# A second dense layer computed by Strassen's seven block products, its output product too

## The chip, the cores and the metric

The kernel runs on one core of one Trainium2 chip. The metric is the device time of one execution in microseconds. Engines of the core are called by the profile's names: PE (matmul) with its weight loads PEld, DVE (vector), ACT (scalar and tables), POOL (GpSimd), and SP, which here issues the DMAs.

## The reference, cut to what matters

```python
# q, k, v: (4, 8, 576, 64) fp32; all weights fp32
attn = softmax(q @ k.T / 8, block-causal mask, blocks of 64) @ v
x = attn.transpose(0, 2, 1, 3).reshape(2304, 512)
h = x @ w_in                       # 512 -> 2048
x = (h - tanh(h)) @ w_out          # 2048 -> 512      "first layer"
xn = x / sqrt(mean(x * x) + 1e-6) * rms_g
g, val = xn @ w_gate, xn @ w_val   # 512 -> 1536 each  "second layer"
out = (g * sigmoid(g) * val) @ w_out2   # 1536 -> 512
```

The weights arrive as float64, so each piece of them (512 numbers a partition, 512 KB) is first converted to fp32 by integer and float operations on DVE and ACT (`convert`).

## The kernel before, in words

**Precision.** Each fp32 operand is held as two fp32r parts, high and low, and each product is three matmuls: high by high, high by low, low by high (`gemm_out`, `product`). Making the two parts is called a split: ACT writes the high part (`rnd`, L100), DVE or POOL subtracts it for the low one (`lo`, L105).

**Tiling.** The 2304 tokens form six groups of 384 (`NG`, `TG`), a group three tiles of 128. The first layer takes group after group; in each, 16 steps (`J1`) of 128 hidden columns: four products of 384 columns for the hidden block (L799 to L801), tanh, and three token tiles' output products of 512 columns into three accumulators (L682 to L684). The attention of later groups is woven between these matmuls by the class `Attn`. In group 0 the first layer's weights are converted; later groups load the split weights again from DRAM copies (`w1d`), two steps ahead, into rings of four buffers.

**The second layer** takes pairs of groups. Its 12 hidden blocks (`J2`) need w_gate, w_val and w_out2. In group 5 of the first layer and in the first pair (`unit_piece`, `unit_sums`, `out_piece`) these are converted: 24 pieces of gate and value weights and 12 of output weights. In the first pair (`plain`) gate and value products are the ordinary ones for each of the two groups. Meanwhile each block's seven Strassen weight combinations are written to DRAM (`w2d`). The second and third pair (`fast`) use them: one hidden block needs 7 block products of 2 x 3 matmuls of 384 columns for both groups together, where the ordinary way needs 8. The Strassen blocks are: rows of the product are gate and value, its columns the two groups. The output product is the ordinary one in all pairs: `out2`, with all 12 split output weight blocks (`wout`) kept in SBUF, 512 columns a matmul, one group first and then the other (`later` holds the second group's hidden blocks until then).

**Order.** PE's order is that of the program text. For the other engines the compiler's scheduler orders instructions, except those pinned (`pin`). Each engine runs its queue in order. All DMAs are issued by SP in one order; an SP entry that waits holds back the ones behind it.

Of the kernel before, what the change touches and what calls it, by code (L numbers as in the profile page):

```python
# [50 lines left out]
EARLYOUT = 6  # L51
LATEOUT = (1, 2, 4, 5, 7, 8)
# [39 lines left out]
def build(ctx, tc, q, k, v, w_in, w_out, w_gate, w_val, w_out2, rms_g, ident_in, out):  # L92
# [19 lines left out]
    w2d = [[drm.tile([128, 2, n], F32, name=f"w2d_{n}_{j}") for j in range(J2)] for n in (768, 1024)]  # L112
# [68 lines left out]
    env["ev"] = wk  # L181
# [393 lines left out]
    with tc.manual_schedule(engines={PE.engine}):  # L575
# [110 lines left out]
        def out1(s, t):  # L686
# [8 lines left out]
            if j == J1 - 1:  # L695
                c = g * TT + t
                x2s = env["ev"].tile([128, DM], F32, name="x2s", tag="x2s")
# [9 lines left out]
        xin = {}  # L707

        def xn_a(n, t):
            c = n * TT + t  # L710
            x = w2a.tile([128, DM], F32, name="xin", tag="xin", bufs=4)
            SP.dma_start(out=x, in_=x2d[c * 128:(c + 1) * 128, :])
            pin(DVE.scalar_tensor_tensor(x, x, rinv[:, c:c + 1], g_bc, ALU.mult, ALU.mult))
            xin[n, t] = x

        def xn_b(n, t):
            x = xin.pop((n, t))
            xh, xl = xt("B", n)
            ps = env["t"].tile([128, 512], F32, name="t", tag="t")
            for kk in range(KD):  # L720
                PE.transpose(ps[:, kk * 128:(kk + 1) * 128], x[:, kk * 128:(kk + 1) * 128], ident)
            tv = ps.rearrange("p (k c) -> p k c", k=KD)
            hv, lv = (a[:, :, t * 128:(t + 1) * 128] for a in (xh, xl))
# [3 lines left out]
        w2 = {}  # L727
        wout = {}
        full = {}

        def out_piece(j):
            pool = w2a if j < EARLYOUT else w2b
            wout[j] = [pool.tile([128, 512], F32R, name=f"wo_{j}_{y}") for y in "hl"]
            convert(stage(rows_(w_out2, j)), *wout[j])

        def unit_piece(j, part):
            if part == 0:
                full[j] = w0.tile([128, 2, 512], F32, name="fu", tag="fu", bufs=4)
            f = full[j]
            convert(stage(cols((w_gate, w_val)[part], j)), f[:, part])  # L740
            if part == 1:
                w2[j] = w = w0.tile([128, 2, 2, 512], F32R, name="wu", tag="wu", bufs=4)
                rnd(ACT, w[:, 0], f)
                lo(DVE, w[:, 1], f, w[:, 0])

        def unit_sums(j):

            f = full.pop(j).rearrange("p g (k c) -> p (g k) c", k=2)
            g_l, g_u, v_l, v_u = (f[:, n] for n in range(4))
            o = w0.tile([128, 4, 256], F32, name="fs", tag="fs")  # L750
            POOL.tensor_tensor(out=o[:, 0], in0=v_u, in1=v_l, op=ALU.add)
            POOL.tensor_tensor(out=o[:, 2], in0=g_u, in1=v_u, op=ALU.subtract)
            POOL.tensor_tensor(out=o[:, 1], in0=o[:, 0], in1=g_u, op=ALU.subtract)
            POOL.tensor_tensor(out=o[:, 3], in0=g_l, in1=o[:, 1], op=ALU.subtract)
            w = w0.tile([128, 2, 4, 256], F32R, name="ws", tag="ws")
            pin(ACT.activation(out=w[:, 0], in_=o, func=AF.Copy))
            lo(DVE, w[:, 1], o, w[:, 0])
            pin(SP.dma_start(out=w2d[0][j], in_=w2[j].rearrange("p x g c -> p x (g c)")[:, :, 0:768].bitcast(F32)))
            SP.dma_start(out=w2d[1][j], in_=w.rearrange("p x g c -> p x (g c)").bitcast(F32))

        pieces = []
        for j in range(4):
            pieces += [lambda j=j: unit_piece(j, 0), lambda j=j: unit_piece(j, 1)]
            if j:
                pieces += [lambda n=n: out_piece(n) for n in ((0, 1), (2, 3), (4, 5))[j - 1]]
# [3 lines left out]
        w2a = None  # L769
        nld = J1  # L770
        for s in range(NSA):
            g, j = divmod(s, J1)
            if j == 0:
                if g == 2:
# [3 lines left out]
                    env["x4"] = x4.__enter__()  # L778
                base, goal = att.pos, att.goal(g)
# [40 lines left out]
            if s:  # L820
# [4 lines left out]
                gts.pop(s - 1)  # L825
            if j == J1 - 1:
                while att.pos < goal:
                    att.step()
                if g == NG - 2:
                    x4.__exit__(None, None, None)  # L830
                    sat.close()
                    sw = ExitStack()
                    w2a = sw.enter_context(tc.tile_pool(name="w2a", bufs=1, side="right"))
                    sw0 = ExitStack()
                    w0 = sw0.enter_context(tc.tile_pool(name="w0", bufs=1, side="right"))
                    env["stg"] = sw0.enter_context(tc.tile_pool(name="st2", bufs=3, side="right"))
                    g_bc = w2a.tile([128, DM], F32, name="g_bc")
                    SP.dma_start(out=g_bc, in_=rms_g.rearrange("(o d) -> o d", o=1).broadcast_to([128, DM]))
                    sev = ExitStack()
                    env["ev"] = sev.enter_context(tc.tile_pool(name="ev", bufs=3, side="right"))  # L840
            if g == NG - 1:
                if j == 5:
                    rms(0, 15)
# [212 lines left out]
```

## Time and profile before

| what | value |
|---|---|
| median of 3 runs | 1082.54 us (1081.65 to 1083.05) |
| the profiled execution | 1080.89 us |
| its span, first to last instruction | 1079.1 us |
| PE busy | 1049.6 us, 97% |
| DVE, ACT, POOL busy | 741.7, 568.2, 253.3 us |
| granted PE clock | 0.995 of 2.4 GHz |
| DMA | 238.43 MB |

Busy shares are means over stages. The stages on the span's clock, read from the last square of each group's output (L700) and PE's first `fast` product of a pair: group 1 of the first layer ends near 257 us, group 2 near 371, group 3 near 463, group 4 near 561, group 5 near 630; the first pair of the second layer ends near 791, the second near 935, the third near 1074, five us before the span's end.

### The profile page before, as it was taken

The page shows a single profiled execution, that of the slowest core. Times are in us where ns is not written, and L with a number is a line of the kernel's source. Part 1 is how long each engine was busy: PE and PEld are TensorE (multiplying, and loading weights), DVE is VectorE, ACT ScalarE, POOL GpSimd, SP SyncE. Part 2 cuts the span into 40 slices and gives each one's busy share as a digit, 9 for nine tenths or more (in the row PEclk, how much of TensorE's full clock was granted, in tenths as well). Part 3 has the DMA queues.
Part 4 walks back from the last instruction along what each step waited for, and adds up shares of the span by engine and source line. Part 5 has one row for each costly group of instructions (what it writes and reads, how often), then busy time and mean ns, then how long its engine had stood idle before and what let it go on. Part 6 is the DMA issues. An engine that isn't in the chain of part 4 may idle for free.

```text
span 1079.1 us, 16811 instructions
## 1 busy us (share of the span) xinstructions
PE 1049.6 (97%) x5588; PEld 932.4 (86%) x5588; DVE 741.7 (69%) x1559; ACT 568.2 (53%) x1307; POOL 253.3 (23%) x372
## 2 busy tenths in 40 slices
PE   7799999999999999999999989999999999999998
PEld 5576668998888999999998979999899998899986
DVE  5888767777777856576657779997455566555552
ACT  5877747667666755476556576563322223322221
POOL 5531201123233223143211013436011021110010
PEclk9999999999999999999999999999999999999999
DMA  9798888978668887775569976894745555154501
GB/s 220 229 292 295 256 292 263 295 209 247 165 176 204 228 236 219 225 227 176 180 228 402 343 263 238 292 327 186 302 151 183 194 205 186 43 216 187 198 24 36
DMA packets 179639, 238.43 MB, mean 221 GB/s; under 512 B 109152, under 2 KB 134368, under 8 KB 174944
## 3 DMA queue, kind: packets, MB, share of 16 engines
q1 hardware_dynamic: 179552, 237.35, 68.2%
q8 instruction: 45, 0.74, 0.3%
q14 instruction: 42, 0.34, 0.1%
HBM read 184.88 MB, written 52.43 MB: 220 GB/s over the span
## 4 chain that ended last, share of the span: by engine, by line
PE 82%; DVE 7%; DMA 4%; ACT 4%; issue 2%; SPq 0%; POOL 0%; DVEq 0%; POOLq 0%; ACTq 0%
PE acc L682 8%; PE acc L684 8%; PE acc L683 8%; PE gv L873 8%; PE gv L872 7%; PE gv L874 7%; PE t L799 5%; PE t L801 5%; PE t L800 5%; PE t L465 5%; PE t L506 3%; PE acc L692 3%; PE t L530 2%; PE t L559 2%; DMA w<-w1d_i 2%
## 5 line engine op out<-in xcount | busy, mean ns | idle before, releaser
L799 PE MATMUL t<-xh,w 128*128 128x384 f32 x384 | 137.8, 359 | 0.0
L801 PE MATMUL t<-xh,w 128*128 128x384 f32 x384 | 129.9, 338 | 0.0
L800 PE MATMUL t<-xl,w 128*128 128x384 f32 x384 | 129.5, 337 | 0.0
L480 ACT ACTIVATE pt<-pt,stat 128x64 f32<-128x64 f32 (+2 forms) x144 | 80.4, 560 | 45.0 <-DVE pt L478 43.7
L100 ACT ACTIVATE gh<-gt 128x384 fp32r<-128x384 f32 x116 | 60.5, 521 | 74.8 <-DVE gt L813 34.7
L682 PE MATMUL acc<-w,gh 128*128 128x512 f32 x240 | 99.1, 413 | 0.3 <-ACT gh L100 0.3
L684 PE MATMUL acc<-w,gl 128*128 128x512 f32 x240 | 95.3, 397 | 1.1 <-DVE gl L105 1.1
L683 PE MATMUL acc<-w,gh 128*128 128x512 f32 x240 | 94.7, 395 | 0.0
L105 DVE TENSOR_TENSOR gl<-gt,gh 128x384 fp32r<-128x384 f32 x116 | 73.5, 633 | 24.3 <-ACT gh L100 24.0
L682 PE MATMUL acc<-wo_h,gh 128*128 128x512 f32 x216 | 85.7, 397 | 0.4 <-ACT gh L100 0.4
L684 PE MATMUL acc<-wo_h,gl 128*128 128x512 f32 x216 | 85.3, 395 | 0.0
L683 PE MATMUL acc<-wo_l,gh 128*128 128x512 f32 x216 | 84.9, 393 | 0.0
L799 PEld LDWEIGHTS t<-xh,w 128*128 128x128 f32 x384 | 72.4, 189 | 3.6 <-issue 0.7
L100 ACT ACTIVATE pp<-t 128x512 fp32r<-128x512 f32 (+6 forms) x152 | 64.2, 437 | 21.1 <-PE t L506 20.4
L478 DVE TENSOR_SCALAR_CACHE_REDUCE pt<-t 128x64 f32<-128x64 f32 (+2 forms) x144 | 64.0, 449 | 16.2 <-PE t L465 15.0
L800 PEld LDWEIGHTS t<-xl,w 128*128 128x128 f32 x384 | 72.5, 189 | 2.2
L801 PEld LDWEIGHTS t<-xh,w 128*128 128x128 f32 x384 | 72.1, 188 | 0.0
L959 POOL TENSOR_TENSOR gs<-c,c 128x384 f32<-128x384 f32 x24 | 24.4, 1015 | 201.4 <-ACT c L958 201.4
L813 DVE TENSOR_TENSOR gt<-t,gt 128x384 f32<-128x384 f32 x80 | 44.2, 553 | 39.5 <-ACT gt L807 39.3
L506 PE MATMUL t<-ident,pt 128*128 128x128 f32 x400 | 65.8, 274 | 3.7 <-POOL pt L493 2.4
L807 ACT ACTIVATE gt<-t 128x384 f32<-128x384 f32 x96 | 46.6, 485 | 40.4 <-PE t L801 40.0
L956 ACT ACTIVATE gt<-c 128x384 f32<-128x384 f32 x24 | 12.6, 526 | 102.1 <-DVE c L955 102.1
(155 smaller groups left out, 2827.4 us busy)
## 6 DMA issues: line engine op xcount, KB each, us to landing
w<-w1d_i SPq DMA_DIRECT2D x80, 512.0 KB, 4.6
w<-w1d_o SPq DMA_DIRECT2D x64, 512.0 KB, 4.3
wb<-w2d SPq DMA_DIRECT2D x24, 1024.0 KB, 4.8
wa<-w2d SPq DMA_DIRECT2D x24, 768.0 KB, 6.3
st<-in_moe_w_out SPq DMA_DIRECT2D x28, 512.0 KB, 4.9
w2d<-ws SPq DMA_DIRECT2D x12, 1024.0 KB, 6.0
w2d<-wu SPq DMA_DIRECT2D x12, 768.0 KB, 5.7
st<-in_moe_w_in SPq DMA_DIRECT2D x16, 512.0 KB, 4.8
```

Source lines behind the costliest of these rows:

```text
L100: ACT.activation(out=o, in_=i, func=AF.Copy)
L480: ACT.activation(out=pt[:, 0:keys], in_=pt[:, 0:keys], func=AF.Exp, scale=-1.0, bias=least, accum_out=st[:, 8 + ti:9 + ti])
L506: PE.transpose(t[:, (j - a) * 128:(j - a + 1) * 128], pt[:, j * 128:(j + 1) * 128], ident)
L682: PE.matmul(acc, lhsT=gh[:, c], rhs=wh, start=first, stop=False)
L683: PE.matmul(acc, lhsT=gh[:, c], rhs=wl, start=False, stop=False)
L684: PE.matmul(acc, lhsT=gl[:, c], rhs=wh, start=False, stop=last)
L799: PE.matmul(h, lhsT=wh[:, c], rhs=xh[:, kk], start=(kk == 0), stop=False)
L800: PE.matmul(h, lhsT=wh[:, c], rhs=xl[:, kk], start=False, stop=False)
L801: PE.matmul(h, lhsT=wl[:, c], rhs=xh[:, kk], start=False, stop=(kk == KD - 1))
L872: PE.matmul(ps, lhsT=wh[:, c], rhs=xh[:, kk], start=(kk == 0), stop=False)
L873: PE.matmul(ps, lhsT=wh[:, c], rhs=xl[:, kk], start=False, stop=False)
L874: PE.matmul(ps, lhsT=wl[:, c], rhs=xh[:, kk], start=False, stop=(kk == nk - 1))
```

## The change

All three pairs now use the seven-product scheme for gate and value (`fast`), and the output product uses it as well (`tail`): over 6 pairs of hidden blocks (`JH`), 7 products of 6 blocks, each for three token tiles with matmuls of 256 columns; the seven left operands are hidden blocks or sums of them made by POOL (`sums`, `sub`), split while the products run; `combine` adds the products into the two groups' outputs on DVE, and half rows of 256 columns are stored. The output weights are no longer held in SBUF: their seven combinations lie in DRAM (`wod`), and each product loads its 6 blocks (1.5 MB) into one of three weight slots (`ws`), which hold the gate and value weights too.

The conversion moves. 11 units (6 of output weights, 5 of gate and value weights; a unit is two pieces, four POOL sums and a split of 1792 columns whose subtraction POOL makes) are converted in groups 2, 3 and 4 of the first layer, as 44 items, four a unit: 10 in group 2, 16 in group 3, 18 in the first 12 steps of group 4; the results are sent to DRAM. The 7 gate and value units of `DIRECT` are converted in group 5 and the first pair, straight into slots or kept buffers; they are written to DRAM for the later pairs (`keep`). The first pair's normalised tokens are loaded, combined and transposed during group 5 (`PREP`).

```diff
+JH = J2 // 2
+DIRECT = (0, 1, 2, 3, 4, 6, 8)
+            def send(self, eng, half):
+                n = slice(3, 7) if half else slice(0, 3)
+                w = env["wsp"].tile([128, 2, 4, 256], F32R, name="wc", tag="wc")[:, :, 0:n.stop - n.start]
+                self.split_part(w, eng, half)
+                if self.kind == "g":
+                    pin(SP.dma_start(out=w2d[self.j][:, :, n], in_=w.bitcast(F32)))
+                    return
+                for y in range(2):
+                    pin(SP.dma_start(out=wod[:, n, self.j, 256 * y:256 * y + 256], in_=w[:, y].bitcast(F32)))
...
+            if 2 <= g < NG - 1:
+                nit = {2: 0, 3: 10, 4: 26}[g] + (j + 1) * {2: 10, 3: 16, 4: 24}[g] // J1
+                while 44 - len(items) < min(nit, 44):
+                    items.pop(0)()
...
-        gvp = ctx.enter_context(tc.tile_pool(name="gvp", bufs=4, space=PSUM))
-        env["t"] = ctx.enter_context(tc.tile_pool(name="tb", bufs=1, space=PSUM))
-        accp = ctx.enter_context(tc.tile_pool(name="accb", bufs=1, space=PSUM))
+        gvp = ctx.enter_context(tc.tile_pool(name="gvp", bufs=8, space=PSUM))
...
+        ORDER = (4, 1, 2, 5, 6, 7, 3)
+        def tail(p):
+            def split(m):
+                i, j = steps[m]
+                f = left[i](j)
+                gh, gl = ([wk.tile([128, TG], F32R, name=n, tag=n) for n in ("gh", "gl")] if m % 2 else
+                          [temp(n, F32R) for n in ("c21", "c22")])
+                rnd(ACT, gh, f)
+                lo(DVE, gl, f, gh)
+                parts.append((gh, gl))
+                if i == 2:
+                    sub(f, f, GS[1][j])
...
+            for n, i in enumerate(ORDER):
+                q = p * NQ + J2 + n
+                load_slot(q + 2)
+                w = slots.pop(q).rearrange("p x n c -> p (x n c)")
+                ps = [bank()[:, 0:256] for t in range(TT)]
+                for j in range(JH):
+                    m = n * JH + j
+                    if m + 3 < len(steps):
+                        split(m + 3)
+                    gh, gl = parts[m]
+                    wh, wl = (w[:, 512 * j + 256 * y:512 * j + 256 * y + 256] for y in range(2))
+                    for t in range(TT):
+                        gemm_out(ps[t], gh, gl, wh, wl, t, j == 0, j == JH - 1)
+                for t in range(TT):
+                    combine(i, t, ps[t])
+                if p + 1 < NG // 2:
+                    if n == 0:
+                        nx = pair_x()
+                    if n < 2:
+                        for k in range(4):
+                            pair_b(n, k, nx, bank)
...
+        for p in range(NG // 2):
+            for j in range(J2):
+                if p or j:
+                    load_slot(p * NQ + j + 2)
...
+                if p == 0:
+                    if j + 3 in direct:
+                        if j + 3 >= 5:
+                            direct[j + 3].piece(1)
+                        direct[j + 3].sums()
+                    if j + 4 in DIRECT[5:]:
+                        direct[j + 4].load()
+                        direct[j + 4].piece(0)
+                fast(p * NQ + j, j, x)
...
+                if j > JH:
+                    if j == JH + 1:
+                        sums(0)
+                    sums(j - JH)
+            x = tail(p)
```

PE, where the first pair goes over to its output products. Before, matmuls of 512 columns into accumulators that stay for twelve blocks:

```order
L682 MATMUL acc_8898<-wo_h,gh 128x512
L683 MATMUL acc_8898<-wo_l,gh 128x512
L684 MATMUL acc_8898<-wo_h,gl 128x512
L682 MATMUL acc_8902<-wo_h,gh 128x512
L683 MATMUL acc_8902<-wo_l,gh 128x512
L684 MATMUL acc_8902<-wo_h,gl 128x512
```

After, matmuls of 256 columns into a bank of the ring `gv`; `ws` is the weight slot, `c` and `gh`/`gl` the two parts of the left operand:

```order
L685 MATMUL gv<-ws,c_8961 128x256
L683 MATMUL gv<-ws,c_8960 128x256
L684 MATMUL gv<-ws,c_8960 128x256
L685 MATMUL gv<-ws,c_8961 128x256
L683 MATMUL gv<-ws,gh 128x256
L684 MATMUL gv<-ws,gh 128x256
```

The first pair has 216 of the former in the one and 378 of the latter in the other; so have the second and the third.

SP, late in group 3 of the first layer. Before, loads of the first layer's weights (`w`) stand among the attention's (`kr`, `qr`, `vr`) alone:

```order
L641 DMA w_5168<-w1d_i_107 128x1024
L270 DMA qr<-in_q 32x6x32 x3
L651 DMA w_5084<-w1d_o_122 128x1024
L270 DMA kr<-in_k 32x18x32 x4
L641 DMA w_5224<-w1d_i_108 128x1024
L651 DMA w_5170<-w1d_o_123 128x1024
```

After, stores of converted combinations (`wod<-wc`) and loads of weights to convert (`st`) stand between them:

```order
L642 DMA w_5624<-w1d_i_100 128x1024
L758 DMA wod<-wc 128x3x256 x2
L652 DMA w_5560<-w1d_o_115 128x1024
L126 DMA st<-in_moe_w_gate 128x4x256
L126 DMA st<-in_moe_w_val 128x4x256
L642 DMA w_5703<-w1d_i_85 128x1024
L652 DMA w_5626<-w1d_o_116 128x1024
```

The store waits for POOL's subtraction into `wc`; the next step's weights are issued behind it.

DVE, in the third hidden block of the first pair. Before, the conversions of gate, value and output weights with the products' multiplications (L911) between them:

```order
L139 TENSOR_SCALAR cv<-cv 128x512
L140 SCALAR_TENSOR_TENSOR cv<-cv,cu 128x512
L141 SCALAR_TENSOR_TENSOR fu<-st,cv 128x512
L911 TENSOR_TENSOR gt<-gv,gt 128x384
L105 TENSOR_TENSOR ws<-fs,ws 128x1024
L105 TENSOR_TENSOR wu<-fu,wu 128x1024
```

After, the subtraction of a unit's split (L739) and the eight operations of `fast` (L1008 to L1019):

```order
L739 TENSOR_TENSOR ws<-fu,ws 128x768
L1008 TENSOR_TENSOR c_8153<-gv,c_8151 128x384
L1009 TENSOR_TENSOR c_8152<-gv,c_8153 128x384
L1013 TENSOR_TENSOR c_8151<-gv,c_8151 128x384
L1011 TENSOR_TENSOR c_8154<-gv,c_8152 128x384
L1012 TENSOR_TENSOR c_8153<-gv,c_8153 128x384
L1015 TENSOR_TENSOR c_8152<-gv,c_8152 128x384
L1018 TENSOR_TENSOR c_8153<-gv,c_8153 128x384
L739 TENSOR_TENSOR ws<-fs,ws 128x1024
L1019 TENSOR_TENSOR g_2_8217<-c_8153,gt 128x384
```

A block of the first pair now has these eight DVE operations in place of two multiplications and a split (`gl`); fewer conversions stand beside them.

## Rows read from the trace of the kernel before

**Rows 1.** The page: busy time by engine, and the chain by engine.
```profile
PE 1049.6 (97%) x5588; PEld 932.4 (86%) x5588; DVE 741.7 (69%) x1559; ACT 568.2 (53%) x1307; POOL 253.3 (23%) x372
...
PE 82%; DVE 7%; DMA 4%; ACT 4%; issue 2%; SPq 0%; POOL 0%; DVEq 0%; POOLq 0%; ACTq 0%
```

**Rows 2.** Windows by stage: stretch, then busy us per engine, clock, DMA share, GB/s.
```profile
257.00:371.00 114.00, 109.77 (x635) 100.41 (x634) 88.54 (x248) 78.57 (x215) 35.27 (x54) 0.99 0.74 195
371.00:463.00 92.00, 92.00 (x504) 84.23 (x503) 57.87 (x137) 53.10 (x124) 24.09 (x36) 1.00 0.83 233
463.00:561.00 98.00, 97.65 (x550) 89.63 (x549) 62.68 (x143) 58.35 (x134) 29.46 (x44) 1.00 0.59 191
561.00:630.00 69.00, 67.62 (x339) 59.57 (x338) 53.74 (x90) 43.93 (x81) 4.03 (x4) 1.00 0.92 344
630.00:791.00 161.00, 157.13 (x842) 146.43 (x841) 125.95 (x172) 85.60 (x146) 56.93 (x56) 1.00 0.73 262
791.00:935.00 144.00, 143.78 (x767) 133.79 (x766) 84.86 (x143) 37.93 (x75) 21.30 (x24) 1.00 0.45 168
935.00:1074.00 139.00, 138.78 (x722) 128.83 (x720) 73.25 (x124) 32.27 (x63) 12.19 (x12) 1.00 0.35 131
```

**Rows 3.** Windows again, of two short stretches where DMA or DVE is fullest.
```profile
570.00:600.00 30.00, 29.50 (x146) 25.82 (x145) 21.15 (x35) 17.95 (x32) 3.19 (x4) 1.00 1.04 402
660.00:690.00 30.00, 30.00 (x166) 29.06 (x165) 29.27 (x38) 18.23 (x31) 13.88 (x12) 1.00 0.90 323
```

**Rows 4.** Timeline of PE near 800 us: start, duration, instruction.
```profile
799.68 0.34 PE L872 MATMUL gv<-xh,wa 128*128 128x384 f32 x1
...
806.51 0.39 PE L682 MATMUL acc<-wo_h,gh 128*128 128x512 f32 x1
...
808.60 0.34 PE L872 MATMUL gv<-xh,wa 128*128 128x384 f32 x1
```

**Rows 5.** Timeline of PE near 766 us, around transposes.
```profile
765.81 1.69 PE L988 MATMUL gv<-ident,xn 128*128 128x128 f32 x14
767.26 0.48 PE L682 MATMUL acc<-wo_h,gh 128*128 128x512 f32 x1
```

**Rows 6.** PE groups by shape: count, busy us, mean ns, idle before.
```profile
L872 PE MATMUL gv<-xh,wb 128*128 128x384 f32 x192 | 64.6, 336 | 0.0
...
L539 PE MATMUL t<-pp,vp 128*128 128x256 f32 x32 | 9.0, 280 | 0.0
```

**Rows 7.** DVE groups by shape.
```profile
L140 DVE SCALAR_TENSOR_TENSOR cv<-cv,cu 128x512 int32<-128x512 int32 x68 | 53.3, 785 | 4.3
...
L139 DVE TENSOR_SCALAR cv<-cv 128x512 f32<-128x512 f32 x68 | 35.8, 527 | 9.5 <-ACT cv L136 8.9
...
L961 DVE TENSOR_TENSOR gt<-c,gt 128x384 f32<-128x384 f32 x24 | 23.2, 967 | 2.5
L105 DVE TENSOR_TENSOR gl<-gs,gh 128x384 fp32r<-128x384 f32 x36 | 21.6, 599 | 36.6 <-ACT gh L100 36.6
...
L141 DVE SCALAR_TENSOR_TENSOR fu<-st,cv 128x512 int32<-128x512 int32 x24 | 17.8, 742 | 0.3
...
L955 DVE TENSOR_TENSOR c<-gv,c 128x384 f32<-128x384 f32 x24 | 13.4, 559 | 0.9
...
L105 DVE TENSOR_TENSOR xl<-gv,xh 128x512 fp32r<-128x512 f32 x18 | 11.3, 685 | 0.9 <-ACT xh L100 0.7
```

**Rows 8.** ACT groups by shape.
```profile
L136 ACT ACTIVATE cv<-st 128x512 f32<-128x512 f32 x68 | 45.4, 667 | 17.6 <-DVE fu L141 6.6 <-DVE wo_l L105 3.2 <-DMA st<-in_moe_w_gate 2.5
...
L100 ACT ACTIVATE wu<-fu 128x1024 fp32r<-128x1024 f32 x12 | 12.7, 1060 | 11.2 <-PE gv L874 5.1 <-issue 4.9 <-DVE fu L141 1.1
```

**Rows 9.** POOL groups by shape.
```profile
L959 POOL TENSOR_TENSOR gs<-c,c 128x384 f32<-128x384 f32 x24 | 24.4, 1015 | 201.4 <-ACT c L958 201.4
...
L751 POOL TENSOR_TENSOR fs<-fu 128x256 f32<-128x256 f32 x12 | 14.0, 1171 | 137.8 <-DVE ws L105 124.0 <-DMA xin<-x2d 13.8
```

**Rows 10.** Timeline of PE near 634 us: the longest wait of the handover.
```profile
636.57 0.66 PE L721 MATMUL t<-ident,xin 128*128 128x128 f32 x4 [2.19 <-DVE xl L105]
```

More of the change, by code (lines that the diff above doesn't have):

```diff
@@ L705, in rms @@
             pin(DVE.reciprocal(rinv[:, a:z], rinv[:, a:z]))
[L707 to L723, printed above, removed]
+        sources = {("g", j): (cols(w_gate, j), cols(w_val, j)) for j in range(J2)}
@@ new lines, in away, with first, second, third @@
+        def away(units, eng):
+            items = []
+            for n, c in enumerate(units):
+                def first(n=n, c=c):
+                    if n == 0:
+                        c.load()
+                    c.piece(0)
+                def second(n=n, c=c):
+                    c.piece(1)
+                    if n + 1 < len(units):
+                        units[n + 1].load()
+                def third(c=c):
+                    c.sums()
+                    c.send(eng, 0)
+                items += [first, second, third, lambda c=c: c.send(eng, 1)]
+            return items
@@ L724, in xn_b @@
             rnd(ACT, hv, tv)
             lo(DVE, lv, tv, hv)
[L727 to L765, printed above, removed]
+        def tbank():
+            return env["t"].tile([128, 512], F32, name="t", tag="t")
+        slots = {}
+        def slot(q):
+            slots[q] = tp.tile([128, 2, 7, 256], F32R, name="ws", tag="ws", bufs=3)
+            return slots[q]
+        items = away([Convert("o", j) for j in range(JH)]
+                     + [Convert("g", j) for j in range(J2) if j not in DIRECT], POOL)
@@ new lines, in build @@
+                    for n in range(3):
+                        items[4 * n + 2] = direct[n].sums
+                        items[4 * n + 3] = lambda n=n: direct[n].split(slot(n), POOL)
+                    items[14:16] = []
+                    items[16:18] = []
+            if g == NG - 1:
+                for k, f in PREP:
+                    if k == j:
+                        f()
+                if j == 14:
+                    direct[0].keep()
+                while len(items) > 16 - (j + 1):
+                    items.pop(0)()
@@ L995, in build @@
[L995 to L1009 removed]
+            POOL.tensor_tensor(out=result(1, j), in0=c12, in1=c22, op=ALU.mult)
@@ new lines, in fast, with sub, sums @@
+            DVE.tensor_tensor(c21, prod(2, xd, 0), c21, ALU.add)
+            DVE.tensor_tensor(result(0, j), c21, gt, ALU.mult)
+        GS = [{}, {}]
+        def sub(o, a, b, op=ALU.subtract):
+            POOL.tensor_tensor(out=o, in0=a, in1=b, op=op)
+        def sums(j):
+            for s in GS:
+                if j not in s:
+                    s[j] = sums_pool.tile([128, TG], F32, name=f"gs{j}_{0 if s is GS[0] else 1}")
+            sub(GS[0][j], G[1][j], G[1][j + JH], ALU.add)
+            sub(G[1][j], G[0][j], G[1][j])
+            sub(GS[1][j], GS[0][j], G[0][j])
@@ L1023, in build @@
[L1023 to L1035 removed]
+                if p == 0 and j == JH:
+                    sw0.close()
+                    sums_pool = sw.enter_context(tc.tile_pool(name="sums", bufs=1, side="right"))
```

331 lines of the change are left out of this document (178 added, 153 removed).

## The prediction

> **What bounds the kernel now.** I read the busy times first, then the chain, then windows cut at the stages, then PE's timeline. PE is busy 97% of the span and is 82% of the chain [rows 1]. A busy PE can still be a slow one, so the cadence is what counts. From the first 384-column matmul shown to the first 512-column one, 39 matmuls start in 6.83 us, 0.175 us each; the nine of 512 columns that follow take 2.09 us, 0.232 each [rows 4]. The windows say where PE stands idle: 4.2 us in group 2, 0.4 in groups 3 and 4, then 1.4 in group 5, 3.9 in the first pair and 0.4 in the two pairs after it [rows 2]. The reader should see that groups 3 and 4 have DVE and ACT at only 58 to 64%, while the first pair has DVE at 78%, and at 98% from 660 to 690 us [rows 3]: room is in the first layer, load is in the first pair. The clock is full in nearly all rows and stays out of the sum. So time goes mostly where PE work goes, plus the waits that the moved conversions make or take away.
>
> **PE work, part by part.** The durations of a group by shape hold the pipeline's depth: 336 ns against a cadence of 175, so 161 ns of depth. A 256-column matmul lasts 280 [rows 6], so its cadence should be 119 ns; I take 0.118.
> - Output product: per pair 216 x 0.232 = 50.1 us becomes 378 x 0.118 = 44.6. That is 5.5 less, three times: -16.5 us.
> - Gate and value of the first pair: 576 matmuls become 504 of 384 columns, 72 x 0.175 = -12.6 us.
> - Transposes of the first pair's tokens: 24 become 42, and 14 take 1.45 us [rows 5], 0.104 each: +1.9 us.
>
> Together -27.2 us. All of it lies on PE, which has no cover to lose, so it is worth its full size wherever PE keeps running.
>
> **Old waits that go.** Four of six output pieces and all splits of output weights leave group 5, and first-pair tokens are transposed well before the handover. The wait of 2.19 us for a token's low part [rows 10] goes with them. I take away the whole idle time of group 5 and the first pair, 1.4 + 3.9 = 5.3 us, and price what comes new in those stages by itself.
>
> **Conversions in groups 2 to 4.** A unit costs DVE two pieces of 0.527 + 0.785 + 0.742 = 4.1 us [rows 7]; ACT two pieces of two reads, each as L136's 0.667, and a split of 1792 columns at 1.06 per 1024, 4.5 us [rows 8]; POOL four sums of 1.17 and 1792 columns at 1.015 per 384, 9.4 us [rows 9]. Eleven units: DVE +45, ACT +50, POOL +103 us. The three groups last 304 us, with DVE at 209, ACT at 190 and POOL at 89 [rows 2]. So DVE goes to 84%, ACT to 79%, POOL to 63%. It is worse locally: group 4 puts its 4.5 units into 12 of 16 steps.
>
> DVE and POOL also get in each other's way. The multiplication at L961 reads two SBUF tiles and runs beside POOL's L959, taking 967 ns; an addition of the same size from PSUM takes 559 [rows 7, 9]. That is 0.41 us a meeting. Some 66 conversion operations and 48 low parts in the three groups, meeting POOL 63% of the time, add 30 us and bring DVE to 93%. The Trainium skill (SBUF — State Buffer, "SBUF: two separate sides") calls the pair's shared port an exclusive lock: a two-input DVE operation and a POOL operation that reads SBUF exclude each other for the whole instruction. By that, a meeting could cost up to a whole POOL operation; the row's 0.41 us is nearer to half of one, and I use the row.
>
> What waits behind such an operation is the chain of a step: tanh on ACT, subtraction on DVE, high part on ACT, low part on DVE, then PE. Also the attention's prepared keys and values on POOL. From below, these waits are nil: at 660 to 690 us DVE was busy 29.27 of 30 us and PE did not stop [rows 3]. From above, take group 2's idle share, 3.7% at DVE 78% [rows 2], doubled for all three groups: 22 us. The prior level of group 2 stays anyway. I take the middle, +11, since the attention's chains in these groups are longer than those at 660 us.
>
> **DMA in these groups.** A unit loads 1.05 MB and writes 1.84. At 2.5, 4 and 4.5 units this adds 63, 125 and 132 GB/s. By group 5's price, share 0.92 for 344 GB/s, the shares become 0.91, 1.16 and 0.94 [rows 2], a mean of 0.995. The fullest stretch held 1.04 with PE busy 29.5 of 30 us [rows 3], so I let the excess of group 3 spill into its neighbours at no price beyond the +11. SP's queue is passed by it: a store of a converted half waits for POOL, and the next step's first-layer weights are issued behind it; they are asked for two steps, some 12 us, ahead. More traffic can't gain anything by itself; from above, the second rival prices it.
>
> **Handover and first pair.** Blocks 1 to 6 give PE 6 x 42 x 0.175 = 44.1 us. DVE has seven additions of 0.559 and one multiplication of 0.967 per block, 29.3 us, four pieces of 2.05, and four splits of 1792 columns at 0.599 per 384, 2.8 each: 48.7 us in all [rows 7]. DVE would be 4.6 us behind PE; eight PSUM banks lend about one block of lead, 7 us. Between 0 and 8 I take +3.
>
> **The new tail.** A product step gives PE 54 x 0.118 = 6.4 us, with transposes 7.8. DVE has six low parts of 0.599, three to six additions of 256 columns (0.37 to 0.56 by the 384-column row, I take 0.42) and, in three of seven steps, four transposed tiles' low parts, 2.5 us [rows 7]. The worst three steps in a row have DVE at about 21.1 us against PE's 20.6. A split is issued three blocks (3.2 us) ahead, which covers ACT and DVE's 1.2 us but not a burst of additions too. +2 us in the first and second pair, none in the third, which transposes nothing: +4, between 0 and 10.
>
> **Hidden.** The slot loads are 1.84 MB per 7.4 us and 1.57 MB per 6.4, about 250 GB/s or a share of 0.67, below the 0.92 that group 5 carried; three slots let a load run two steps ahead. If that cover failed, each late load would cost a step's remainder, some 2 us. Weights for the output product no longer sit in SBUF, which costs these loads alone.
>
> **Sum.** -27.2 - 5.3 + 11 + 3 + 4 = -14.5 us. The profiled execution of 1080.9 us (span 1079.1 and 1.8 around it, which I leave) becomes 1066.4. That execution lies 1.7 us under the median of the runs shown, and just below the fastest of them; between 1066.4 and 1068.1 I say 1067.
>
> **Rivals.**
> 1. No new waits: every moved operation is hidden, as at 660 to 690 us. For it speaks that row, and that groups 3 and 4 leave PE idle for 0.4 us. Against it, group 2 waits already at 78%. 1080.9 - 32.5 = 1048.4; 1046 to 1057.
> 2. The DMA queue decides, and it gets slower. The queue's demand in groups 2 to 4 is 0.995 x 304 = 302.5 us of full share. The most that a stage with attention loads carried is 0.83 (group 3), the most of any stage 0.92 [rows 2]. At the middle, 0.875, the groups take 346 us, 42 more; first-layer weights come late and PE stands. -32.5 + 42 + 7 = +16.5: 1097. It decides for slower from a ceiling under about 0.92, where the 25.5 us that the rest saves are gone. Against it: 1.04 was held for 30 us [rows 3].
> 3. Narrow matmuls don't pay: a weight load comes with each matmul, and the output product has 75% more of them. The bounds are 0.104, a transpose of 128 columns [rows 5], and 0.232, no saving at all. At their middle, 0.168, the output product takes 63.5 us a pair, 13.4 more instead of 5.5 less: +57 on the forecast, 1123. Against it stands the 280 ns of the row [rows 6]. The Trainium skill (TensorE: Matmul & The Clock Gate, "Back-to-back issue gap") says that weight load and matmul set the spacing together, and gives sustained 81 ns at 128 columns and 131 at 512: by interpolation, an estimate, 98 at 256, three quarters of the price of 512, which would make it 1128. Its 131 does not agree with the 232 of rows 4.
>
> **How the numbers follow.** Forecast, 1057 to 1078: 0.52. Rival 1: 0.26. Rival 2, 1078 and up: 0.18, of which 0.05 falls within 0.2% of no change (about what a measurement of this kernel can tell). Rival 3: 0.04. Faster 0.78, same 0.05, slower 0.17. Range: below 1048 lies some 0.05 of rival 1; above 1092 half of rival 2 and rival 3. 1048 to 1092 leaves out under 0.2; the forecast's own range is 1057 to 1078.
>
> **What would show it.** In the new profile: 1134 matmuls of 256 columns at a cadence near 118 ns; the second and third pair near 139 and 134 us in place of 144 and 139; the first pair near 141 in place of 161; groups 2 to 4 some 11 us longer than 304, with DVE over 85%, PE idle there about 15 us and its waits ended by DVE, ACT or POOL. Were those waits ended by DMA of `w`, rival 2 is at work; were there none, rival 1. The forecast is wrong if the first layer, whose end moves from 630 us by +11, -1.4 and thirty more transposes' 3.1 us to some 643, ends before 636 or after 650 us.

## The result: slower by 1.1%, and the profile after

The changed kernel takes 1095.39 us (median of 4 runs, 1093.96 to 1097.14) against 1082.80 us for the kernel before beside it: a ratio of 1.0113, 95% interval 1.0089 to 1.0137. The prediction was 1067 us, and faster; it was wrong by 28 us and in its sign. The profiled execution took 1095.53 us, its span is 1093.7 us.

The page of the changed kernel, busy time by engine and the chain by engine (answers to [rows 1]):

```profile
PE 1039.3 (95%) x6020; PEld 943.4 (86%) x6020; DVE 844.5 (77%) x1714; ACT 602.4 (55%) x1390; POOL 442.6 (40%) x529
...
PE 71%; DVE 12%; ACT 6%; DMA 5%; issue 4%; POOL 1%; SPq 1%; DVEq 0%; ACTq 0%; POOLq 0%
```

PE has fewer busy microseconds than before, and yet the end comes later: the chain now runs 12% over DVE. The windows by stage of the changed kernel say where (groups 2, 3, 4, 5, then the three pairs; columns as in [rows 2]):

```profile
257.00:386.00 129.00, 118.99 (x654) 108.06 (x652) 107.86 (x268) 89.92 (x234) 53.58 (x72) 0.93 0.82 228
386.00:487.00 101.00, 94.89 (x499) 84.43 (x500) 83.00 (x163) 66.48 (x147) 48.52 (x53) 0.98 1.04 303
487.00:599.00 112.00, 103.82 (x555) 92.75 (x554) 82.71 (x159) 73.33 (x159) 62.01 (x69) 0.97 0.82 272
599.00:675.00 76.00, 69.89 (x348) 61.31 (x347) 55.97 (x81) 42.35 (x78) 42.17 (x37) 0.96 0.85 308
675.00:815.00 140.00, 137.57 (x923) 137.01 (x922) 120.16 (x203) 63.20 (x121) 69.40 (x67) 1.00 0.81 301
815.00:955.00 140.00, 137.57 (x922) 137.00 (x922) 106.83 (x176) 47.15 (x96) 53.70 (x51) 1.00 0.70 253
955.00:1088.00 133.00, 132.35 (x879) 132.14 (x878) 93.19 (x159) 41.95 (x84) 42.63 (x39) 1.00 0.67 239
```

Against [rows 2] the three pairs are 21, 4 and 6 us shorter: the second layer, from there to the span's end, lasts 419 us where it lasted 449. Groups 2 to 4 last 342 us where they lasted 304, group 5 some 7 us more. So the whole loss lies in the first layer, and 38 us of it where the moved conversions are. Of those 38, PE's idle time explains 19.7 (10.0 + 6.1 + 8.2 against 4.2 + 0 + 0.4). The granted clock explains up to 13 more: 129 us at 0.93, 101 at 0.98 and 112 at 0.97 lack 14.4 us of full speed, where before 114 us at 0.99 lacked 1.1. That is an estimate from rounded shares, and some of the slow time was idle and is counted twice. The last 5 us or so lie in busy time that these views do not divide.

What PE waited for in groups 2 to 4, before and after (instruction, releaser: us in total, times, the longest). Before:

```profile
PE t L530 <- DVE pp L105: 2.3, 3, 1.7
PE t L539 <- DVE pp L105: 1.3, 2, 1.0
PE t L465 <- DVE pp L105: 1.0, 1, 1.0
```

After:

```profile
PE acc L685 <- DVE gl L105: 10.1, 7, 3.4
PE t L466 <- DVE pp L105: 3.4, 1, 3.4
PE t L531 <- DVE pp L105: 2.7, 3, 1.2
PE t L466 <- DVE avt L534: 2.1, 1, 2.1
```

Four smaller ones follow, 5.8 us together; DVE ends all but one of 1.1 us, which POOL ends. None is ended by a DMA, though the DMA share of group 3 is 1.04. One such wait, by the timelines of POOL, of DVE and of PE in the changed kernel near 428 us (start, duration, instruction, idle before and its releaser):

```profile
427.27 2.37 POOL L739 TENSOR_TENSOR wc<-fs,wc 128x1024 fp32r<-128x1024 f32 x1 [1.89 <-ACT wc L738]
```

```profile
427.34 2.85 DVE L141 SCALAR_TENSOR_TENSOR cv<-cv,cu 128x512 int32<-128x512 int32 x1
430.11 0.55 DVE L105 TENSOR_TENSOR gl<-gt,gh 128x384 fp32r<-128x384 f32 x1
```

```profile
428.03 0.39 PE L684 MATMUL acc<-w,gh 128*128 128x512 f32 x1
430.71 0.50 PE L685 MATMUL acc<-w,gl 128*128 128x512 f32 x1 [2.29 <-DVE gl L105]
```

POOL starts a moved split's subtraction. A DVE operation on SBUF that starts 0.07 us later, and takes 0.69 us undisturbed, lasts 2.85 us and ends 0.55 us behind POOL's: it got hardly anything done before POOL was through. The step's low part `gl` is queued behind it, and PE stands for 2.29 us. That is the theory of the experiments: a long POOL operation holds DVE for its whole length, and what stands behind it on DVE is a link between two matmuls.

### The profile page after: what moved, and what is told of

The parts are those of the page before. It is cut to its first block, busy times and chain, and to the rows that moved or that the text cites. A ratio compares the mean times of both kernels' runs of the same rounds, so it can differ in the third digit from the quotient of the medians.

```text
span 1093.7 us, 18315 instructions
## 1 busy us (share of the span) xinstructions
PE 1039.3 (95%) x6020; PEld 943.4 (86%) x6020; DVE 844.5 (77%) x1714; ACT 602.4 (55%) x1390; POOL 442.6 (40%) x529
## 4 chain that ended last, share of the span: by engine, by line
PE 71%; DVE 12%; ACT 6%; DMA 5%; issue 4%; POOL 1%; SPq 1%; DVEq 0%; ACTq 0%; POOLq 0%
PE gv L961 8%; PE gv L963 8%; PE gv L962 8%; PE gv L685 4%; PE t L873 4%; PE gv L684 4%; PE gv L683 4%; PE t L874 4%; PE t L875 4%; PE acc L685 3%; PE acc L683 3%; PE t L466 3%; PE acc L684 3%; PE acc L693 3%; PE t L560 2%
## 5 line engine op out<-in xcount | busy, mean ns | idle before, releaser
L961 PE MATMUL gv<-xh,ws 128*128 128x384 f32 x504 | 169.0, 335 | 1.0 <-DVE x2s L102 1.0
L963 PE MATMUL gv<-xh,ws 128*128 128x384 f32 x504 | 169.2, 336 | 0.0
L962 PE MATMUL gv<-xl,ws 128*128 128x384 f32 x504 | 169.0, 335 | 0.0
L685 PE MATMUL acc<-w,gl 128*128 128x512 f32 x240 | 99.2, 413 | 12.8 <-DVE gl L105 12.8
L1017 POOL TENSOR_TENSOR g<-c,c 128x384 f32<-128x384 f32 x36 | 40.5, 1124 | 165.9 <-ACT c L1016 160.1
L683 PE MATMUL acc<-w,gh 128*128 128x512 f32 x240 | 101.3, 422 | 2.4 <-ACT gh L100 2.4
L1014 ACT ACTIVATE gt<-c 128x384 f32<-128x384 f32 x36 | 18.9, 525 | 144.0 <-DVE c L1013 144.0
L684 PE MATMUL acc<-w,gh 128*128 128x512 f32 x240 | 97.1, 405 | 0.0
L961 PEld LDWEIGHTS gv<-xh,ws 128*128 128x128 f32 x504 | 94.6, 188 | 1.4 <-ACT sq L701 1.4
L963 PEld LDWEIGHTS gv<-xh,ws 128*128 128x128 f32 x504 | 94.6, 188 | 0.0
L962 PEld LDWEIGHTS gv<-xl,ws 128*128 128x128 f32 x504 | 94.6, 188 | 0.0
L105 DVE TENSOR_TENSOR gl<-gt,gh 128x384 fp32r<-128x384 f32 x80 | 60.8, 761 | 15.0 <-ACT gh L100 14.8
```

The source lines that it names most:

```text
L683: PE.matmul(acc, lhsT=gh[:, c], rhs=wh, start=first, stop=False)
L684: PE.matmul(acc, lhsT=gh[:, c], rhs=wl, start=False, stop=False)
L685: PE.matmul(acc, lhsT=gl[:, c], rhs=wh, start=False, stop=last)
L961: PE.matmul(ps, lhsT=wh[:, c], rhs=xh[:, kk], start=(kk == 0), stop=False)
L962: PE.matmul(ps, lhsT=wh[:, c], rhs=xl[:, kk], start=False, stop=False)
L963: PE.matmul(ps, lhsT=wl[:, c], rhs=xh[:, kk], start=False, stop=(kk == nk - 1))
```

## The experiments

In the expectations theory A is this one (holding), theory B is that DVE is simply given too much work; traffic is the other rival. "Moved units" are the eleven of groups 2 to 4. Diffs are against the changed kernel where nothing else is said. Ratios are to the kernel before, run beside on the same chip, with 95% intervals.

**Everything moved is left out.**

```diff
-                while 44 - len(items) < min(nit, 44):
-                    items.pop(0)()
...
```

> The 11 units of groups 2 to 4 are left out (loads, conversion, sums, split, stores); the slots that would hold them are loaded with other blocks of the same size, so the second layer does all its work on wrong weights. Theories: (A) lock: POOL's long SBUF operations, the splits' subtractions of 768 and 1024 columns above all, hold up DVE's SBUF operations, and PE waits for the late low parts. (B) load: DVE and ACT simply have more to do in their in-order queues. (C) DMA: the stores and loads fill the queue. All three expect the 37 us that groups 2 to 4 lost (342 in place of 304) to come back: 1095 - 37 = 1058 us, PE idle in these groups near 5 us. If the second layer's gain of 29 us were an artefact, it would show as over 1070.

Measured: 1057.10 us (1055.01 to 1057.74), ratio 0.9769 (0.9752 to 0.9785). Its windows of groups 2 to 4:

```profile
259.00:374.00 115.00, 110.76 (x640) 100.72 (x639) 89.41 (x249) 80.80 (x220) 35.74 (x56) 0.99 0.74 195
374.00:465.00 91.00, 91.00 (x498) 83.40 (x499) 56.45 (x134) 52.37 (x122) 25.26 (x36) 1.00 0.83 231
465.00:562.00 97.00, 96.65 (x543) 88.59 (x542) 61.38 (x139) 57.38 (x132) 27.80 (x41) 1.00 0.63 202
```

These are the stages of before. Without the moved conversions the change is worth 24.8 us, and they cost 1095.4 - 1057.1 = 38.3 us (37 by the two ratios, which take out the difference between chips): more than all that the change gains.

**POOL's part of them left out** (high part stored twice, no sums, no subtraction; all traffic, DVE's and ACT's conversions stay).

```diff
-                self.split_part(w, eng, half)
+                pin(ACT.activation(out=w[:, 0], in_=x, func=AF.Copy))
...
-                    c.sums()
...
```

> The units of groups 2 to 4 keep their loads, their DVE and ACT conversion, the ACT half of the split and the same bytes of stores, but POOL's four sums and its two subtractions are left out (the high part is stored twice). (A) lock: DVE's excess over its undisturbed durations in groups 2 to 4 (48 us) falls to near the 12 of before, PE's waits go: 1062 to 1072 us. (B) load: DVE and ACT have the same instructions: 1088 to 1096. (C) DMA: same bytes: 1092 to 1096.

Measured: 1074.47 us (1073.45 to 1078.78), ratio 0.9935 (0.9912 to 0.9957). POOL's work is worth 20.9 of the 38.3 us, 2.5 us above the range of theory A and far below those of (B) and (C). In groups 2 to 4 of this kernel's trace the granted clock is back at 0.99, 1.00 and 1.00.

**The moved subtractions on DVE**, the whole computation.

```diff
-                     + [Convert("g", j) for j in range(J2) if j not in DIRECT], POOL)
+                     + [Convert("g", j) for j in range(J2) if j not in DIRECT], DVE)
```

> The splits' subtractions of the 11 units are made by DVE in place of POOL (22 operations of 0.9 to 1.2 us, +24 us of DVE work); POOL keeps the sums of 0.74 us. Nothing is left out. (A) lock: the longest holders are gone, DVE's excess halves or better: 1070 to 1083 us. (B) load: DVE has 24 us more to do in 342: 1097 to 1108. (C) DMA: 1093 to 1097.

Measured: 1078.39 us (1074.39 to 1083.90, 10 runs), ratio 0.9969 (0.9947 to 0.9990). The engine that is said to be full gets 22 operations more, and the kernel gets 17 us faster. DVE's busy time in groups 2 to 4 even falls, from 273.6 to 270.7 us. That rules out theory B as the main cause. What stays are PE's waits in groups 2 to 4, of the profiled execution of this kernel (1081.84 us, 3.5 above the median):

```profile
PE t L466 <- DVE pp L105: 4.4, 2, 3.4
PE acc L685 <- DVE gl L105: 3.5, 4, 1.7
PE t L540 <- DVE pp L105: 3.3, 4, 1.5
PE t L531 <- DVE pp L105: 2.1, 3, 1.3
```

`gl` falls from 10.1 to 3.5 us; the attention's `pp` does not fall.

**The subtraction in pieces of 256 columns**, on POOL as in the change.

```diff
-                eng.tensor_tensor(out=w[:, 1], in0=x, in1=w[:, 0].bitcast(F32), op=ALU.subtract)
...
+                for b in range(4 if half else 3):
+                    eng.tensor_tensor(out=w[:, 1, b], in0=x[:, b], in1=w[:, 0, b].bitcast(F32), op=ALU.subtract)
```

> POOL makes each subtraction of a split in pieces of 256 columns (3 and 4 in place of 1), all else the same. (A) lock, if the length of one holding decides: no DVE operation is held longer than some 0.75 us at once, PE's waits shrink: 1080 to 1090 us. (A'), if the held time as a whole decides: 1093 to 1098. (B) and (C): 1093 to 1097.

Measured: 1089.55 us (1087.67 to 1091.47), ratio 1.0067 (1.0048 to 1.0085). The same subtractions in shorter pieces give 5.8 us back: the length of one holding matters. They give back a third of what moving them to DVE does. That pieces in a row hold DVE too would fit, but no run separates it.

**POOL's subtractions alone, put into the kernel before**: 22 of 768 or 1024 columns on scratch data, at the places of the change.

```diff
...
+                while done < nit:
+                    if done % 4 > 1:
+                        cn = 768 if done % 4 == 2 else 1024
+                        ACT.activation(out=sc[:, 0, 0:1], in_=gt[:, 0:1], func=AF.Copy)
+                        POOL.tensor_tensor(out=sc[:, 1, 0:cn], in0=sc[:, 0, 0:cn], in1=sc[:, 1, 0:cn], op=ALU.subtract)
+                    done += 1
...
```

> The kernel before, with nothing changed but 22 POOL subtractions of 768 and 1024 columns on scratch tiles in groups 2 to 4 of the first layer, at the places where the moved units have theirs (and an ACT copy of one column ahead of each, 0.2 us, which times them). Nobody waits for their results. (A) lock: DVE's excess in these groups rises by 12 to 20 us and the time from 1082 to 1087 to 1094 us. (B) and (C): at most ACT's 4 us of copies show, 1081 to 1084.

Measured: 1093.95 us (1092.28 to 1094.84) against 1082.67, ratio 1.0107 (1.0085 to 1.0130). Nothing in this kernel needs these results, DVE and DMA get no work, ACT gets 22 copies of one column, and it loses 11.3 us. Its windows of groups 2 to 4, and the low part `gl` of 257 to 599 us in it (least, median and longest duration in ns):

```profile
257.00:377.00 120.00, 114.55 (x650) 102.80 (x649) 96.93 (x253) 81.54 (x227) 43.80 (x58) 0.99 0.72 190
377.00:471.00 94.00, 92.11 (x501) 83.43 (x500) 61.69 (x134) 52.94 (x129) 43.49 (x44) 1.00 0.82 225
471.00:572.00 101.00, 98.68 (x550) 89.10 (x549) 69.54 (x143) 58.27 (x144) 50.45 (x54) 1.00 0.58 185
```

```profile
L105 DVE TENSOR_TENSOR gl<-gt,gh x55: 530/557/2541, 259.4 to 599.0; 128x384 fp32r<-128x384 f32 x55
```

DVE's busy time in groups 2 to 4 rises from 209.1 [rows 2] to 228.2 us with nothing but 22 operations on POOL and as many on ACT added; 8.4 us of that lie in group 2, where four of the 22 stand. Which operations of DVE grow tells the mechanism. Two of DVE's groups by shape in groups 2 to 4, before and then in this kernel (count, busy us, mean ns); `gl` is the difference of two tiles of SBUF, `gt` that of a tile of PSUM and one of SBUF:

```profile
L105 DVE TENSOR_TENSOR gl<-gt,gh 128x384 fp32r<-128x384 f32 x49 | 30.3, 618 | 4.9 <-ACT gh L100 4.7
L813 DVE TENSOR_TENSOR gt<-t,gt 128x384 f32<-128x384 f32 x48 | 26.5, 552 | 22.0 <-ACT gt L807 21.8
```

```profile
L105 DVE TENSOR_TENSOR gl<-gt,gh 128x384 fp32r<-128x384 f32 x49 | 39.6, 808 | 4.9 <-ACT gh L100 4.7
L818 DVE TENSOR_TENSOR gt<-t,gt 128x384 f32<-128x384 f32 x48 | 26.4, 550 | 18.5 <-ACT gt L812 18.4
```

The one grows by 190 ns in the mean, the other keeps its time to 2 ns: a DVE that was merely late or full would not do this. Nor does this trace speak for POOL's own attention work, late behind the added operations: every wait of PE in these groups is ended by DVE. So the run shows by itself that long POOL operations hold DVE and cost PE time. Its size is only in part divided: PE's idle time rises by 5.1 us, the clock stays at 0.99, 1.00 and 1.00, and the other 6 us lie in PE's busy time.

**No moved subtraction and no sums on POOL** (DVE subtracts; the sums of the moved units are left out).

```diff
...
-                    c.sums()
...
+                     + [Convert("g", j) for j in range(J2) if j not in DIRECT], DVE)
```

> As e3 (subtractions of the splits on DVE), and POOL's four sums of 256 columns per moved unit are left out (the split works on unsummed blocks). (A) lock: the 44 sums of 0.74 us still held DVE; its excess in groups 2 to 4 falls from 29 us to near 18, and the time from 1078 to 1069 to 1074 us. If only long holdings hurt: 1076 to 1080.

Measured: 1076.70 us (1072.93 to 1079.20, 10 runs), ratio 0.9948 (0.9932 to 0.9964). That is 1.7 us under the kernel with the sums, within the uncertainty, and in the range for "only long holdings hurt": sums of 0.74 us each cost next to nothing.

**No POOL work and no stores** of the moved units.

```diff
...
-                for y in range(2):
-                    pin(SP.dma_start(out=wod[:, n, self.j, 256 * y:256 * y + 256], in_=w[:, y].bitcast(F32)))
...
```

> As e2 (no POOL work in the moved units), and the 20 MB of stores of these units are left out too; later loads read other blocks of the same size. What is left of the moved conversions is their loads, and DVE's and ACT's part. e2 took 1074.5 us, e1 without any of it 1057.1: 17 us are still to be placed. If DMA (C) carries them: 1060 to 1068 us. If DVE's and ACT's load (B) does: 1072 to 1077.

Measured: 1071.13 us (1068.21 to 1073.39), ratio 0.9897 (0.9867 to 0.9927): 3.3 us under the kernel without POOL's work, with intervals that overlap, and between the two ranges, nearer to that of (B). The stores are no main cause.

**No POOL work and no conversion** (ACT writes the raw words; loads and stores stay).

```diff
...
-                    c.piece(0)
...
-                    c.piece(1)
...
+                pin(ACT.activation(out=w[:, 0].bitcast(I32), in_=x, func=AF.Copy, scale=LOWBITS, bias=-0.5))
```

> As e2 (no POOL work in the moved units), and their conversion on DVE and ACT (six DVE and four ACT operations a unit) is left out; ACT writes the tile that is stored from the raw bits, loads and stores stay. What is left of the moved conversions is all of their DMA and two ACT operations a unit. If DVE's and ACT's load (B) carries the 17 us between e1 and e2: 1058 to 1064 us. If DMA (C) does: 1070 to 1075.

Measured: 1065.51 us (1063.79 to 1069.54), ratio 0.9852 (0.9822 to 0.9881). That is 1.5 us above the range of (B) and well below that of (C). So, left out in this order, the 38.3 us divide into 20.9 for POOL's operations, 9.0 for the conversions of DVE and ACT, and 8.4 for what is left, traffic and ACT's copies, which no run separates; by the ratios 19, 9 and 9.

**The subtractions of group 5 on DVE too**, the whole computation.

```diff
...
-                        items[4 * n + 3] = lambda n=n: direct[n].split(slot(n), POOL)
+                        items[4 * n + 3] = lambda n=n: direct[n].split(slot(n), DVE)
```

> The changed kernel with the split subtractions of the eleven moved units and of the three direct units of group 5 on DVE; the whole computation. Theory A (what costs is DVE held through a whole long POOL operation): group 5 still lies 3 us over the kernel without moved conversions in the run that moved only the eleven units' subtractions (78 us of stretch against 72 to 74), so 2 to 4 us come back from 1078.4: 1073 to 1078. Theory B (DVE is merely full, each operation more lengthens its queue): group 5 gets 5.4 us more DVE work and the time rises, 1079 to 1084.

Measured: 1079.04 us (1074.67 to 1080.90, 11 runs), ratio 0.9966 (0.9952 to 0.9980). Nothing came back: a miss of theory A by 1 us, at the lower end of B. In group 5, without attention, it made no measurable difference whether POOL or DVE did the six operations.

**The sums on DVE too**, the whole computation, so that POOL does nothing for a moved unit.

```diff
...
-                    c.sums()
+                    c.sums(eng)
...
```

> The changed kernel with both the split subtractions and the four sums of each moved unit on DVE, so that POOL does nothing for a moved unit; the whole computation. The sums are 44 operations of 256 columns, 0.4 to 0.6 us of DVE each, 18 to 26 us more DVE work in groups 2 to 4. Theory A: leaving the sums out altogether was worth 1.7 us, so their holding is worth no more than that, while DVE has idle time for most of 18 us: 1074 to 1081. Theory B (load): DVE in these groups goes from about 280 to about 300 us of 320 and PE's waits grow, 1085 or more.

Measured: 1083.62 us (1080.27 to 1091.19, 10 runs), ratio 1.0016 (0.9997 to 1.0035). Between the two ranges: 5 us worse than with the sums on POOL. Load on DVE has a price after all, some 5 us for these 44 operations.

**The items laid out otherwise**, with all subtractions on DVE: none in group 2, 18 in group 3, 26 in group 4.

```diff
...
-                nit = {2: 0, 3: 10, 4: 26}[g] + (j + 1) * {2: 10, 3: 16, 4: 24}[g] // J1
+                nit = {2: 0, 3: 0, 4: 18}[g] + (j + 1) * {2: 0, 3: 18, 4: 26}[g] // J1
...
```

> As the kernel with all split subtractions on DVE, and the 44 items given out as none in group 2, 18 in group 3 and 26 in group 4 (the change gave 10, 16 and 18); the whole computation. Group 2 was 14 us longer with its 10 items than without any moved conversion, although it has the fewest; groups 3 and 4 were 8 and 2 us longer with 34. If the place decides (group 2 has its attention's DVE work, 78% busy before): group 2 gives 12 to 14 us back, groups 3 and 4 pay 3 to 8 more, 1066 to 1072. If each item costs the same wherever it stands (24 us over 44 items), nothing changes: 1073 to 1078.

Measured: 1086.90 us (median of eleven: ten from 1084.39 to 1090.41 and one of 3559.97, which is not in the ratio), ratio 1.0039 (1.0025 to 1.0052): slower, and neither expectation had it. Group 2 gave its loss back (it ends at 374 us), but a new wait came at the handover. Windows of this kernel behind group 4, two of several, and the wait:

```profile
590.00:600.00 10.00, 10.00 (x56) 9.16 (x55) 8.60 (x11) 5.57 (x11) 6.74 (x7) 1.00 1.03 419
...
650.00:667.00 17.00, 3.49 (x12) 3.52 (x13) 14.80 (x20) 9.97 (x18) 8.53 (x8) 0.60 0.68 223
```

```profile
PE gv L961 <- DVE x2s L102: 14.4, 1, 14.4
```

The queue of DMAs stays at 1.03 to 1.05 from 578 to 630 us. From 650 us on, DVE's queue holds conversions of direct units ahead of the first layer's last results (`x2s`), and PE stands 14.4 us.

**A milder layout**: 4, 18 and 22 items, group 5's subtractions on POOL.

```diff
...
-                nit = {2: 0, 3: 10, 4: 26}[g] + (j + 1) * {2: 10, 3: 16, 4: 24}[g] // J1
+                nit = {2: 0, 3: 4, 4: 22}[g] + (j + 1) * {2: 4, 3: 18, 4: 28}[g] // J1
```

> As the kernel with the eleven units' split subtractions on DVE (1078.4 us), with the 44 items given out as 4 in group 2, 18 in group 3 and 22 in the first 13 steps of group 4; the whole computation. With none in group 2 that group gave its 14 us back, but group 4 with 26 items in 16 steps ran 8 us longer, and the queue of DMAs stayed full into group 5, where loads and conversions came late and PE waited 14 us at the handover. If that late end was the trouble, and each group has some room of its own: group 2 gives 4 to 8 us back, group 4 pays 2 to 4, the handover nothing: 1072 to 1077. If the total of DVE work and traffic in the three groups is what counts, wherever it stands: 1077 to 1082.

Measured: 1088.03 us (1085.92 to 1090.00, 6 runs), ratio 1.0052 (1.0033 to 1.0071). Both expectations missed. The first layer ends 8 us earlier than with the change's layout and DVE's subtractions (653 against 661 us), and the first pair loses more than that. Its window and PE's waits there:

```profile
653.00:700.00 47.00, 38.59 (x193) 35.91 (x192) 41.09 (x61) 25.45 (x42) 27.18 (x23) 0.89 0.80 292
```

```profile
PE gv L961 <- ACT ws L738: 4.4, 2, 2.9
PE gv L963 <- POOL ws L739: 2.8, 3, 1.8
```

PE now waits for the direct units' own splits, 7.2 us in these two lines, and the granted clock is 0.89 there. Why these come late is not settled: the scheduler's order of the unpinned instructions moves with the items, and I made no experiment on that.

The version that beats both kernels is therefore the plain one: the moved subtractions on DVE, 1078.4 us, and as good with those of group 5 there too, 1079.0; 0.3% under the kernel before.

## Why the prediction was wrong, point by point

**The step that failed is "Conversions in groups 2 to 4", the term +11 with bounds 0 and 22.** It measured 38.3 us. The sum without it was -25.5 us; measured without the conversions, -24.8 (interval -27 to -23). So nearly the whole error is in this one term, and in it at the step from DVE's busy time to PE's waits. Four things were wrong in that step.

- *A mean in place of a length.* I took 0.41 us a meeting from a mean [rows 7]. As a sum it served well: it put DVE at 209 + 45 + 30 = 284 us in these groups, and DVE was busy for 273.6; the time for which DVE was held rose from 12 to 48 us, by 36 where I had 30. What a mean cannot tell is how long one holding lasts. I set aside the rule that I had cited (the Trainium skill, SBUF — State Buffer, "SBUF: two separate sides": the shared port is locked for the whole instruction). The runs agree with the rule: beside 2.37 us of POOL, 0.69 us became 2.85. The lengths of the moved operations, POOL's groups of the changed kernel by shape (count, busy us, mean ns):

```profile
L739 POOL TENSOR_TENSOR wc<-fs,wc 128x1024 fp32r<-128x1024 f32 x11 | 26.5, 2413 | 15.4 <-ACT wc L738 12.8 <-issue 1.8 <-POOL xs L535 0.7
...
L739 POOL TENSOR_TENSOR wc<-fu,wc 128x768 fp32r<-128x768 f32 x11 | 20.4, 1853 | 6.3 <-ACT wc L738 6.3
```

The trace of before could have told it, by the longest in place of the mean. In it, the durations of `gl` from 257 to 599 us (least, median, longest), and the timelines of POOL and of DVE around that longest one:

```profile
L105 DVE TENSOR_TENSOR gl<-gt,gh x57: 518/555/1609, 258.3 to 595.8; 128x384 fp32r<-128x384 f32 x57
```

```profile
263.12 1.56 POOL L105 TENSOR_TENSOR vp<-vr,vp 128x640 fp32r<-128x640 f32 x1 [0.15 <-ACT vp L100]
```

```profile
263.49 1.61 DVE L105 TENSOR_TENSOR gl<-gt,gh 128x384 fp32r<-128x384 f32 x1 [1.20 <-ACT gh L100]
```

DVE's operation starts 0.37 us into POOL's and ends 0.42 us behind its end: it was held for most of the rest of POOL's time. A mean over those that met and those that did not hides this. With operations of 1.9 and 2.4 us the median of `gl` stays at 555 ns, and its longest grows from 1609 to 2443; of all DVE operations in groups 2 to 4, 18 lasted over 1 us longer than is usual for their shape, where 2 did before. The row from 660 to 690 us, from which I took that waits can be nil, had twelve POOL operations in 13.88 us [rows 3], 1.2 us each, and could not show this.

- *From DVE's load to PE's wait.* I predicted DVE at 93% of 304 us; it is at 80% of 342. The chains broke before DVE was full: PE waits for the one low part that stands behind a held operation, not for the mean. Its waits for `gl` alone are 10.1 us, where the list of before has none. "Take group 2's idle share, doubled" was no upper bound, since an idle share at one load says nothing of a new length of single holdings.

- *The clock.* "The clock is full in nearly all rows and stays out of the sum" held before and broke after: up to 13 of the 38 us, as estimated above. It came with the waits: without POOL's operations the clock was back.

- *What is not POOL's.* POOL's operations are 20.9 us of the term. The other 17 came without them, 9.0 with the conversions on DVE and ACT and 8.4 with traffic and ACT's copies, so that these too exceed the +11; I had given traffic "no price beyond the +11".

**PE work, -27.2: right.** The output product's cadence after, two rows of PE's timeline:

```profile
795.76 0.28 PE L685 MATMUL gv<-ws,gl 128*128 128x256 f32 x1
...
798.85 0.28 PE L684 MATMUL gv<-ws,c 128*128 128x256 f32 x1
```

26 steps lie between them in 3.09 us, 0.119 each, for the 0.118 taken. Rival 3 is ruled out. (Its 1128 should have been 1129 or 1130 by its own figures; nothing hangs on it.)

**Handover, first pair, new tail: right to 1 us.** Predicted 141, 139 and 134 us for the pairs, measured 140, 140 and 133. By the sum's own terms the second should have read 144 - 5.5 + 2 = 140.5. These are sums of a stage: no run measured the +3 and the +4 apart.

**Group 5**: forecast at 69 - 1.4 + 3.1 = 70.7 us, measured 76, and 73 without the moved conversions. So the old wait taken away there, -1.4, did not come back as a gain.

**The DMA queue.** Rival 2 named 1097 us, close to the result, but not by its mechanism: share 1.04 was held through group 3 with every wait of PE ended by an engine. The experiments leave it at most 8.4 us, so that its number was near is luck. In the layout without items in group 2 the queue was full to 630 us, but PE's long wait there was ended by DVE; whether late loads lay behind it is not shown.

**Rival 1** (no new waits, 1048) is refuted by the waits shown above.

**The marks set for the new profile**: first layer over before 650 us, measured 675, so the forecast was called wrong by its own mark; groups 2 to 4 longer by 38 and not 11; DVE there 80%, under the 85 predicted; PE idle 24.3 us where 15 was said; the releasers, DVE above all, as said.

## What to carry to other kernels

Before giving POOL a job because it is idle, ask how long a single instruction of it will be and what is queued on DVE at that time: if a low part between two matmuls can come behind it, put it on DVE itself (17 us back here) or cut it (6 us back). Look for such a cost in the longest duration that a held operation shows in the trace and in the length of the new operation, not in a mean over all of them. And a PE that stands for some microseconds may be charged again in clock, as in groups 2 to 4 here: look at the granted clock behind the longest waits that the trace has.

## What the runs showed of the hardware that was not expected

**The clock after a wait.** In the changed kernel PE waited 2.15 us before 296.94 us, 1.46 and 0.62 us near 317 us, and 2.29 us before 430.71 us. The windows behind these three (the third figure from the end is the granted clock):

```profile
297.00:303.00 6.00, 4.84 (x16) 4.29 (x17) 4.54 (x15) 2.09 (x7) 1.72 (x5) 0.50 0.86 207
317.00:324.00 7.00, 6.38 (x22) 5.66 (x22) 4.89 (x14) 3.69 (x10) 0.00 (x0) 0.53 0.71 181
430.00:437.00 7.00, 6.22 (x31) 5.45 (x32) 6.47 (x15) 2.08 (x6) 3.29 (x4) 1.00 1.11 257
```

Behind the first two the clock is at its lower level, 1.2 GHz, for some 6 us, which costs half of that each time; behind the third it stays at 2.4 GHz. What tells them apart these runs do not show. In the ten runs of the kernel with DVE's subtractions time and clock go together: 1074.39 us at a mean clock of 0.993, 1083.90 at 0.982.

**An operation with one input is held too.** The changed kernel's L140 reads one tile of SBUF and writes one. Its durations from 257 to 599 us (least, median, longest), and the timelines of POOL and of DVE around the longest:

```profile
L140 DVE TENSOR_SCALAR cv<-cv x21: 398/420/2511, 266.5 to 597.8; 128x512 f32<-128x512 f32 x21
```

```profile
530.00 2.40 POOL L739 TENSOR_TENSOR wc<-fs,wc 128x1024 fp32r<-128x1024 f32 x1
```

```profile
530.18 2.51 DVE L140 TENSOR_SCALAR cv<-cv 128x512 f32<-128x512 f32 x1 [0.89 <-ACT cv L137]
```

It ends 0.29 us behind POOL's operation and lasts six times its median. The prediction had told the rule for two-input operations alone; this one reads no second tile.

**Operations that do nothing for anyone cost time**: 22 POOL subtractions, 50.6 us of POOL that no engine waits for, made the kernel before 11.3 us longer.
